# A low part made by an adding transfer, one chunk's convolution on VectorE, and a new order of work, in a gated-attention kernel

## The chip, the core and the metric

The kernel runs on one core of a Trainium2 chip. The core's engines run side by side, each from a queue of its own in program order: PE (TensorE: matrix products; its weight loads are shown as PEld), DVE (VectorE), ACT (ScalarE), POOL (GpSimd) and SP (SyncE, which here only issues transfers). They wait for one another through semaphores. SBUF is the memory on the chip that all of them read and write; PSUM is the one that PE writes into, in eight banks. The metric is the device time of one execution in microseconds (us), as the median of several.

## What is computed

A linear attention with a gated state (4 sequences, 8 heads, 768 steps, head size 48) feeds a gated projection of width 384:

```python
f = 1.0 / (1.0 + np.exp(-f_logit))
for t in range(S):
    state = f[:, :, t, :, None] * state + np.einsum('bhd,bhe->bhde', k[:, :, t], v[:, :, t])
    y[:, :, t] = np.einsum('bhd,bhde->bhe', q[:, :, t], state)
...
for k in range(K):                      # K = 5
    gate_pre += conv_w[k][None, None, :] * xp[:, k:k + S, :]
gate = 1.0 / (1.0 + np.exp(-gate_pre))
val = x @ w_val
return (gate * val @ w_out).astype(np.float32)
```

`x` is the attention's output with the heads side by side, and `xp` is `x` with four zero rows ahead of it.

## The kernel before, in words

The 768 steps are cut into six chunks of 128. For each chunk the kernel makes running sums of the gate's logarithms, exponentials of them (`exp1`, `exp2`), scaled keys and queries (`pmulk`, `pmulq`), the scores of a sequence against itself within the chunk (`scores`, from chunk 2 on `scoresq`, which leaves out a quarter that the mask makes zero), the mask (`mask`, on DVE), the product with the values (`apply`, `applyq`), the part that comes from the state (`cross`, `crossb`), and the state's update (`ktrans`, `kevac`, `dstate`, `stadd`, `stmul`). Halves of this work write to one PSUM bank from two groups of PE's rows: between the two, POOL writes one element (`mark`), which waits for PE's first group and for which PE's second group waits (`pairwise`).

`xevac` copies the attention's output from PSUM into `XF`, a buffer per chunk (two of them, in turn), with four columns ahead of it that hold the end of the chunk before (`halo`). From there the second half, the projection, starts. Its work is cut into the units of `UNITS`: units 0 and 1 are chunk 0's first and last two sequences, units 2, 3, 4 and 5 are chunks 1, 2, 3 and 4, and units 6 and 7 are the halves of chunk 5. So `mval 2 1` is output block 1 of chunk 1.

PE multiplies in a reduced 32-bit form, so each operand is split into two parts, high and low, and three of the four products are added up: high by high, high by low, low by high. For `x`, `msplit` (ACT) rounds `XF` into `xH`, and `mlow` (DVE) subtracts: `xL` = `XF` - `xH`, 128 partitions by 1536 elements for a whole chunk. `mval` (PE) multiplies both parts with the parts of `w_val` into PSUM. The gate is a convolution with five taps and a sigmoid, made in one of two ways:

- chunks 0 and 1: `conv` on PE (`mconv`), twelve small products of 32 by 32 per tap with the diagonal weights in `wd`, and then `gate` on ACT, which reads PSUM;
- from chunk 2 on: for each of three blocks of 128 channels, `mlast` (ACT) writes the last tap times `x` into `gt`, four `mtap` (DVE) add the other taps, and `gate` (ACT) makes the sigmoid in place.

`mmul` (DVE) multiplies value and gate, `mhigh` (ACT) and `mrest` (DVE) split the result, `mout` (PE) multiplies with `w_out`, and `mstore` copies to SBUF and stores.

For PE's convolution, the channels of `x` stand in turned groups of 32 (`TURN`, `place`). `CS` says from which chunk on they stand unturned: 2 before. At that chunk `halo` goes through five transfers of SP that turn the groups, elsewhere through one copy on DVE; and from it on `mval` uses a turned copy of `w_val` (`wvHt`, `wvLt`), which `wturn` makes by transfers.

The order in which all of these steps are written is a string, `PROGRAM`: every step names its chunk or unit and its part. `Ordered` gives each engine its instructions in just that order. The weights are made from 64-bit words along the way (`weight`, on POOL, ACT and DVE), and `busy` runs idle products on PE at the start.

Of the kernel before, what the change touches and what calls it, by code (L numbers as in the profile page):

```python
# [33 lines left out]
CS = 2  # L34
# [20 lines left out]
halo 0; loadf 0 0; loadf 0 1; loadq 0 0; loadv 0 0; loadk 0 0; loadk 0 1; loadk 0 2; wload 0; loadf 1 1; pexp 0 0;  # L55
loadv 0 1; pln 0 0; busy 6; cum 0 0; loadq 0 1; pexp 0 2; loadq 0 2; loadf 1 0; pln 0 2; wload 1; exp2 0 0; busy 2;
cum 0 2; exp1 0 0; pmulk 0 0; pexp 0 1; wload 2; pmulq 0 0; loadv 0 2; pln 0 1; ktrans 0 0; exp2 0 2; cum 0 1;
loadk 1 0; weight 0; loadq 1 0; scores 0 0; kevac 0 0; pmulk 0 2; loadf 2 0; exp1 0 2; dstate 0 0; mask 0 0;
exp2 0 1; ktrans 0 2; loadv 1 0; ktrans 0 3; exp1 0 1; pmulk 0 1; kevac 0 2; apply 0 0; weight 0; pexp 1 1; okc 0;
pmulq 0 1; ktrans 0 1; pmulq 0 2; xevac 0 0; scores 0 1; pln 1 1; weight 0; weight 0; weight 0; weight 0;  # L60
kevac 0 1; taps; cum 1 1; loadq 2 0; kevac 0 3; pexp 1 0; loadk 2 0; mask 0 1; pln 1 0; dstate 0 1; scores 0 2;
exp2 1 1; stadd 0 0; cum 1 0; exp1 1 1; mask 0 2; weight 2; weight 2; weight 2; apply 0 1; exp2 1 0;
weight 2; scores 0 3; weight 2; loadv 2 0; xevac 0 1; msplit 0; weight 2; dstate 0 2; loadq 2 1; exp1 1 0;
mask 0 3; weight 1; dstate 0 3; loadk 2 1; apply 0 2; weight 2; stadd 0 1; apply 0 3; weight 1; pmulk 1 0;
xevac 0 2; loadf 3 0; xevac 0 3; weight 1; ktrans 1 1; msplit 1; conv 0 0; weight 1; kevac 1 1; weight 1;
conv 0 1; pmulq 1 0; loadv 2 1; conv 0 2; pmulk 1 1; cross 1 0; pexp 2 0; weight 1; scores 1 0; okc 1; halo 1;
mlow 1; ktrans 1 0; conv 0 3; mask 1 0; weight 2; pln 2 0; conv 0 4; pmulq 1 1; scores 1 1; kevac 1 0; gate 0 2;
scan 2 0; dstate 1 1; loadk 3 0; dstate 1 0; apply 1 0; gate 0 0; mask 1 1; weight 4; gate 0 1; cross 1 1;
weight 1; ktrans 1 3; stadd 1 0; weight 4; wturn 0; scores 1 2; mlow 0; exp2 2 0; weight 4; apply 1 1;
# [10 lines left out]
applyq 2 0; mhigh 1 2; mrest 0 2; mhigh 1 1; mrest 1 2; mhigh 0 1; mrest 1 1; gate 2 2; scan 4 1; loadq 4 0;  # L80
xevac 2 1; mout 1 1; loadv 4 0; stmul 2 0; mrest 0 1; mrest 0 0; mout 1 0; pmulq 2 1; mstore 1 1; gate 2 1; mout 0 2;
xevac 2 0; okc 2; pmulq 3 0; mstore 1 0; gate 2 0; scoresq 2 2; mstore 0 2; mmul 2 1; cross 2 1; pmulq 3 1; mout 0 1;
mask 2 2; mout 1 2; mstore 0 1; scan 4 0; scoresq 2 3; mstore 1 2; mout 0 0; loadk 4 1; mask 2 3; exp2 4 0; mval 2 0;
pmulk 3 1; exp2 4 1; scoresq 3 3; pmulk 4 0; applyq 2 1; mstore 0 0; mmul 2 0; exp1 4 1; pmulk 4 1; exp1 4 0;
ktrans 4 1; mhigh 2 1; okc 4; pmulq 4 0; loadv 4 1; stmul 2 1; loadq 4 1; ktrans 3 2; ktrans 4 0; mask 3 3;
xevac 2 3; ktrans 4 2; loadf 5 0; xevac 2 2; mval 2 2; mrest 2 1; mhigh 2 0; halo 3; kevac 3 2; mrest 2 0; mlast 3 1;
mlast 3 0; mtap 3 1 0; scoresq 3 0; msplit 3; mmul 2 2; dstate 3 2; mtap 3 0 0; ktrans 3 1; ktrans 3 3; kevac 4 2;
mask 3 0; ktrans 3 0; kevac 3 1; kevac 3 3; dstate 4 2; mtap 3 0 1; kevac 3 0; dstate 3 1; mhigh 2 2; dstate 3 3;
mtap 3 0 2; dstate 3 0; kevac 4 1; scoresq 3 1; stadd 3 1; pexp 5 0; mrest 2 2; ktrans 4 3; mtap 3 0 3; loadk 5 0;
mout 2 1; mask 3 1; kevac 4 3; mlast 3 2; mlow 3; kevac 4 0; pln 5 0; mout 2 2; mtap 3 2 0; mtap 3 2 1; gate 3 0;  # L90
mval 3 0; mtap 3 2 2; mtap 3 2 3; mstore 2 2; scan 5 1; gate 3 2; mout 2 0; mstore 2 1; mmul 3 0; exp2 5 1;
scoresq 4 1; scan 5 0; dstate 4 3; dstate 4 0; cross 3 0; exp1 5 1; applyq 3 0; stadd 3 0; mtap 3 1 1; exp2 5 0;
mtap 3 1 2; exp1 5 0; mtap 3 1 3; mval 3 2; loadq 5 0; mask 4 1; xevac 3 0; loadv 5 0; gate 3 1; pmulk 5 0;
scoresq 3 2; mmul 3 2; xevac 3 1; dstate 4 1; okc 5; mhigh 3 0; check; loadk 5 1; mval 3 1; mstore 2 0; mrest 3 0;
stmul 3 0; mask 3 2; mhigh 3 2; stadd 4 0; scoresq 4 0; mmul 3 1; cross 3 1; mrest 3 2; mhigh 3 1; applyq 3 1;
mask 4 0; mrest 3 1; pmulk 5 1; mout 3 2; xevac 3 3; loadv 5 1; pmulq 4 1; xevac 3 2; loadq 5 1; mlast 4 2; halo 4;
mlast 4 1; pmulq 5 0; mout 3 1; mlast 4 0; mtap 4 1 0; stmul 3 1; mtap 4 0 0; msplit 4; mtap 4 0 1; mout 3 0;
pmulq 5 1; mstore 3 1; mstore 3 2; mlow 4; scoresq 5 0; cross 4 0; mstore 3 0; stadd 4 1; applyq 4 0; mtap 4 1 1;
mtap 4 1 2; mtap 4 1 3; mval 4 0; stmul 4 0; mask 5 0; mtap 4 2 0; xevac 4 0; gate 4 1; mtap 4 2 1; cross 5 0;
xevac 4 1; mtap 4 2 2; scoresq 4 3; mtap 4 2 3; mval 4 2; mask 4 3; gate 4 2; mtap 4 0 2; mtap 4 0 3; scoresq 4 2;  # L100
mmul 4 2; gate 4 0; count; mval 4 1; mask 4 2; mhigh 4 2; mmul 4 0; mrest 4 2; mhigh 4 0; scoresq 5 3; mmul 4 1;
cross 4 1; mrest 4 0; mhigh 4 1; applyq 4 1; mrest 4 1; mout 4 1; stmul 4 1; mask 5 3; xevac 4 2; xevac 4 3;
mout 4 2; mlast 5 2; halo 5; msplit 5; mtap 5 2 0; mtap 5 2 1; mlast 5 1; cross 5 1; mlow 5; scoresq 5 2; mstore 4 1;
mlast 5 0; mout 4 0; mstore 4 2; mask 5 2; mtap 5 2 2; mtap 5 1 0; applyq 5 1; mstore 4 0; mtap 5 1 1; mtap 5 2 3;
mtap 5 1 2; gate 5 2; mval 5 1; mtap 5 1 3; xevac 5 2; xevac 5 3; mtap 5 0 0; gate 5 1; mlast 7 2; mtap 5 0 1;
msplit 7; mval 5 0; mtap 5 0 2; mlast 7 1; mmul 5 1; mlast 7 0; mtap 7 1 0; mhigh 5 1; mlow 7; mval 5 2; mtap 5 0 3;
mrest 5 1; gate 5 0; mtap 7 2 0; mval 7 0; mmul 5 0; mmul 5 2; mhigh 5 0; mval 7 2; mtap 7 2 1; mhigh 5 2; mrest 5 0;
scoresq 5 1; mrest 5 2; mval 7 1; mtap 7 2 2; mask 5 1; mout 5 2; mtap 7 2 3; mtap 7 0 0; gate 7 2; mtap 7 0 1;
mmul 7 2; mtap 7 0 2; mhigh 7 2; applyq 5 0; mtap 7 0 3; mstore 5 2; mrest 7 2; mtap 7 1 1; gate 7 0; mtap 7 1 2;
# [31 lines left out]
def gla_moe(ctx: ExitStack, tc: tile.TileContext, q, k, f, v, wv, cw, wo, ft, out):  # L141
# [475 lines left out]
    def mhigh(w, m):  # L617
        ACT.copy(w["gH"][:, m], w["gt"][:, m])
# [291 lines left out]
```

## Time and profile before

| | |
|---|---|
| median of 3 runs | 194.4 us (193.73 to 194.59) |
| profiled execution, whole time | 193.15 us |
| its span, first to last instruction | 191.5 us |
| granted clock of PE, mean | 0.995 |
| transfers | 32.64 MB in 12522 packets |

The profile is one execution. A group row gives engine, operation, tile written and tiles read (`xL<-xf,xH`), shape and count, then the busy time in us and the mean of one in ns, then the engine's idle time ahead of it and what ended that. A row of sums by stretch gives the busy time of each engine between two times. A timeline row gives start and duration in us. In all of them a helper's line (L129, now L131) stands for every recorded operation, so rows are told apart by their tiles. PE's operations are pipelined: one record's duration overlaps the next, and what a step of PE takes is read from one start to the next.

### The profile page before, as it was taken

The page shows a single profiled execution, that of the slowest core. Times are in us where ns is not written, and L with a number is a line of the kernel's source. Part 1 is how long each engine was busy: PE and PEld are TensorE (multiplying, and loading weights), DVE is VectorE, ACT ScalarE, POOL GpSimd, SP SyncE. Part 2 cuts the span into 40 slices and gives each one's busy share as a digit, 9 for nine tenths or more (in the row PEclk, how much of TensorE's full clock was granted, in tenths as well). Part 3 has the DMA queues.
Part 4 walks back from the last instruction along what each step waited for, and adds up shares of the span by engine and source line. Part 5 has one row for each costly group of instructions (what it writes and reads, how often), then busy time and mean ns, then how long its engine had stood idle before and what let it go on. Part 6 is the DMA issues. An engine that isn't in the chain of part 4 may idle for free.

```text
span 191.5 us, 8303 instructions
## 1 busy us (share of the span) xinstructions
PE 180.2 (94%) x3706; PEld 144.8 (76%) x3706; DVE 162.2 (85%) x233; ACT 144.8 (76%) x284; POOL 13.7 (7%) x42
## 2 busy tenths in 40 slices
PE   3999999979999999999899999999999999999990
PEld 1888876667987458888698777888778778988990
DVE  7359899977998999969899997999994699998930
ACT  5889896988979998569999989394634947339440
POOL 6000110242000320000000000000000000000000
PEclk9999999999999999999999999999999999999998
DMA  5999999997647232644912308444000040010322
GB/s 194 344 419 416 416 415 409 415 349 245 203 114 285 41 113 62 206 128 135 350 48 104 113 12 266 130 183 156 15 3 3 3 167 3 3 54 4 140 87 65
DMA packets 12522, 32.64 MB, mean 170 GB/s; under 512 B 3008, under 2 KB 5440, under 8 KB 11456
## 3 DMA queue, kind: packets, MB, share of 16 engines
q1 hardware_dynamic: 12048, 31.65, 46.6%
q8 instruction: 31, 0.51, 1.2%
q10 hardware_dynamic: 432, 0.39, 0.7%
q14 instruction: 11, 0.09, 0.2%
HBM read 26.51 MB, written 4.72 MB: 163 GB/s over the span
## 4 chain that ended last, share of the span: by engine, by line
PE 56%; DVE 19%; ACT 13%; issue 6%; DMA 3%; POOL 0%; ACTq 0%; DVEq 0%
PE bk L129 49%; PE aps L129 8%; DVE re L129 7%; DVE gt L129 5%; ACT ss L129 4%; DMA out<-osb 3%; ACT e L129 2%; ACT xf L129 2%; DVE asb L129 2%; DVE qb L129 1%; DVE rg L129 1%; DVE xL L129 1%; ACT osb L129 1%; DVE rqb L129 1%; ACT re L129 1%
## 5 line engine op out<-in xcount | busy, mean ns | idle before, releaser
L129 ACT ACTIVATE e<-e 112x512 f32<-112x512 f32 (+4 forms) x38 | 36.6, 997 | 4.1 <-DMA e<-in_ft 2.0
L129 PE MATMUL bk<-rg,woH 128*128 128x512 f32 (+1 forms) x108 | 30.1, 365 | 0.1
L129 DVE TENSOR_TENSOR asb<-aps,tri 128x768 f32<-128x768 f32 (+1 forms) x24 | 24.9, 1039 | 5.4 <-PE aps L129 4.0
L129 DVE SCALAR_TENSOR_TENSOR gt<-xf,cws,gt 128x512 f32<-128x512 f32 x36 | 26.5, 748 | 1.5 <-ACT gt L129 0.9
L129 PEld LDWEIGHTS aps<-qb,kb 48*64 48x64 f32 (+1 forms) x640 | 19.9, 144 | 7.3 <-issue 4.8
L129 PE MATMUL bk<-asb,vb 128*32 128x64 f32 (+2 forms) x1280 | 24.4, 232 | 0.4 <-issue 0.4
L129 PE MATMUL aps<-qb,kb 48*64 48x128 f32 (+2 forms) x640 | 23.7, 257 | 0.1
L129 PEld LDWEIGHTS bk<-asb,vb 128*32 128x32 f32 (+1 forms) x1280 | 20.0, 108 | 4.1 <-issue 1.1
L129 PEld LDWEIGHTS bk<-rg,woH 128*128 128x128 f32 x108 | 18.6, 188 | 4.3 <-issue 0.8
L129 DVE TENSOR_TENSOR kb<-kb,e 112x1024 f32<-112x1024 f32 (+1 forms) x13 | 14.8, 1137 | 6.0 <-DMA kb<-in_k 3.5
L129 PE MATMUL bk<-rg,woL 128*128 128x512 f32 (+1 forms) x54 | 19.4, 358 | 0.0
L129 ACT ACTIVATE ss<-u,e 112x48 f32<-112x48 f32 x64 | 15.3, 324 | 3.9 <-PE bk L129 3.9
L129 DVE TENSOR_TENSOR_SCAN e<-keep,e 112x1024 f32<-112x1024 bf16 x8 | 18.3, 2282 | 0.0
L129 PE MATMUL bk<-qb,ss 48*32 48x128 f32 x640 | 15.8, 275 | 1.5 <-ACT cb L129 1.2
L129 ACT COPY osb<-bk 128x512 f32<-128x512 f32 (+1 forms) x20 | 9.8, 495 | 9.1 <-DMA out<-osb 7.3
L129 DVE TENSOR_TENSOR qb<-qb,e 112x1024 f32<-112x1024 f32 (+1 forms) x13 | 14.8, 1146 | 0.0
L129 ACT COPY xf<-bk 128x384 f32<-128x384 f32 x24 | 10.8, 473 | 4.6 <-PE bk L129 4.6
L129 PEld LDWEIGHTS bk<-qb,ss 48*32 48x32 f32 x640 | 10.6, 106 | 4.6 <-issue 1.4
L129 PE MATMUL bk<-xH,wvH 128*128 128x256 f32 (+1 forms) x36 | 13.3, 370 | 0.4 <-ACT xf L129 0.4
L129 PE MATMUL bk<-xL,wvH 128*128 128x256 f32 (+1 forms) x36 | 12.2, 339 | 0.0
L129 PE MATMUL bk<-xH,wvL 128*128 128x256 f32 (+1 forms) x36 | 12.1, 337 | 0.0
L129 ACT CAST rg<-gt 128x512 fp32r<-128x512 f32 (+1 forms) x18 | 9.3, 546 | 3.7 <-DVE gt L129 3.7
(107 smaller groups left out, 343.0 us busy)
## 6 DMA issues: line engine op xcount, KB each, us to landing
kb<-in_k SPq DMA_DIRECT2D x9, 512.0 KB, 5.2
qb<-in_q SPq DMA_DIRECT2D x9, 512.0 KB, 4.5
e<-in_f SPq DMA_DIRECT2D x4, 1024.0 KB, 10.2
vb<-in_v SPq DMA_DIRECT2D x9, 448.0 KB, 4.9
out<-osb SPq DMA_DIRECT2D x12, 256.0 KB, 2.4
raww<-in_wv SPq DMA_DIRECT2D x1, 1152.0 KB, 9.0
raww<-in_wo SPq DMA_DIRECT2D x1, 1152.0 KB, 11.8
kb<-in_k SPq DMA_DIRECT2D x1, 1024.0 KB, 14.1
```

The lines of the kernel that those rows point to most:

```text
L129: ins = emit(*a, **kw)
```

## The change

`CS` goes from 2 to 1: chunk 1's gate is no longer made by `conv` on PE but by `mlast` on ACT and `mtap` on DVE, chunk 1's `x` stands unturned, and the turning halo and the turned `w_val` serve from chunk 1 on.

For units 2 to 5 (chunks 1 to 4) `mlow` is replaced by two steps: `mneg` (ACT) writes the negative of `xH` into `xL`, and `mlowd` is a transfer, issued by POOL, that adds `XF` to it. Units 0, 1, 6 and 7 keep `mlow`. Two further functions of this kind, `mrneg` and `mrestd`, are defined and not used.

`PROGRAM` is written anew from the first step to the last. `busy` now stands three times, with 6, 3 and 3 products (6 and 2 before).

```diff
-CS = 2
+CS = 1
...
-dstate 2 1; stadd 2 1; conv 2 0; pmulq 2 0; exp1 3 1; conv 2 1; stadd 2 0; msplit 2; scan 3 0; scoresq 2 1;
...
+mask 2 0; weight 4; cross 2 0; exp2 3 1; stadd 2 1; scoresq 2 2; mlowd 2; stadd 2 0; scan 3 0; mhigh 1 1;
...
+    def mneg(w):
+        ACT.activation(w["xL"], w["xH"].bitcast(F32), AF.Copy, scale=-1.0)
+
+    def mlowd(w):
+        POOL.dma_start(w["xL"].bitcast(F32), w["xf"][:, :, w["b"], HALO:], accum_op=ALU.add)
...
+        "mneg": lambda n: mneg(view(n)), "mlowd": lambda n: mlowd(view(n)),
```

More of the change, by code (lines that the diff above doesn't have):

```diff
@@ L65 @@
[L65 to L69, printed above, removed]
@@ L80 @@
[L80 to L84, printed above, removed]
@@ L85 @@
[L85 to L109, printed above, removed]
@@ new lines @@
+gate 2 1; mtap 2 0 3; mout 0 1; mtap 2 2 0; mval 2 2; mtap 2 2 1; gate 2 0; mstore 0 1; mtap 2 2 2; xevac 2 3;
+stmul 2 1; mmul 2 1; mout 1 2; mmul 2 0; mtap 2 2 3; mout 1 0; mstore 1 2; loadf 5 0; okc 3; pmulk 3 1; xevac 2 2;
+gate 2 2; scoresq 3 0; mhigh 2 1; mmul 2 2; ktrans 3 1; mstore 1 0; mask 3 0; ktrans 3 3; mhigh 2 0; ktrans 3 0;
+mhigh 2 2; ktrans 3 2; mrest 2 0; kevac 3 0; scoresq 3 1; mrest 2 2; kevac 3 2; kevac 3 1; cross 3 0; mrest 2 1;
+kevac 3 3; loadk 5 0; dstate 3 1; mlast 3 0; mask 3 1; mout 2 1; mlast 3 2; mtap 3 0 0; msplit 3; mtap 3 2 0;
@@ new lines @@
+dstate 4 2; mneg 5; scoresq 5 1; mrest 4 0; stadd 4 1; mout 4 2; okc 5; check; mlast 5 1; mlowd 5; mlast 5 0;
+mtap 5 1 0; stmul 4 1; mtap 5 0 0; count; mout 4 0; mtap 5 1 1; mtap 5 1 2; mstore 4 2; mlast 5 2; mtap 5 1 3;
+mout 4 1; mstore 4 0; mtap 5 2 0; gate 5 1; mask 5 1; mtap 5 2 1; cross 5 1; mstore 4 1; scoresq 5 0; mtap 5 2 2;
+mtap 5 2 3; applyq 5 1; mtap 5 0 1; gate 5 2; mask 5 0; mtap 5 0 2; mval 5 2; xevac 5 2; mtap 5 0 3; xevac 5 3;
+mlast 7 2; gate 5 0; mtap 7 2 0; mlast 7 1; mtap 7 2 1; mval 5 1; mlast 7 0; mtap 7 2 2; msplit 7; mmul 5 2;
```

83 lines of the change are left out of this document (58 added, 25 removed).

## The prediction

> **What bounds the kernel now.** I read the page's busy times first, then the sums by stretch, then the tail of the timeline.
>
> ```profile
> span 191.5 us, 8303 instructions
> PE 180.2 (94%) x3706; PEld 144.8 (76%) x3706; DVE 162.2 (85%) x233; ACT 144.8 (76%) x284; POOL 13.7 (7%) x42
> 0.00:50.00 50.00, 45.25 (x812) 35.27 (x813) 39.90 (x60) 42.44 (x76) 9.47 (x24) 1.00 0.94 358
> 50.00:184.00 134.00, 132.05 (x2873) 106.78 (x2872) 122.35 (x174) 101.19 (x206) 4.27 (x18) 1.00 0.32 104
> 186.64 0.28 PE L129 MATMUL bk<-rkb,woL 128*128 128x256 f32 x1
> 182.55 0.98 DVE L129 TENSOR_TENSOR rqb<-re,rkb 128x256 fp32r<-128x256 f32 x2
> ```
>
> The sums by stretch give, after the bounds and the length, the busy time of PE, PEld, DVE, ACT and POOL, then the granted clock, the DMA share and GB/s. In the first 50 us the loads set the pace: the DMA share is 0.94 and PE idles 4.75 us. From 50 to 184 us PE is busy 132.05 of 134 us, idle 1.5%; DVE is busy 122.35 and idles 11.65 us (8.7%). The last matmul ends at 186.9, 3.4 us after DVE's last operation; then come the copy, the store and the end of the program. So from 50 us on PE is the bound, DVE comes second, and ACT third with 101.19. A change wins what it takes from PE, as long as DVE can run with less idle time than now.
>
> All sums go against the profiled execution, 193.15 us (span 191.5 and 1.65 around it). The median of the runs shown is 194.4, 1.25 above it; I add each difference to 194.4.
>
> **The change part by part.** *Chunk 1's convolution leaves PE.*
>
> ```profile
> 61.00 2.22 PE L129 MATMUL bk<-xf,wd 32*32 32x512 f32 x48
> L129 PE MATMUL bk<-xf,wd 32*32 32x512 f32 x240 | 11.0, 597 | 0.0
> L129 DVE SCALAR_TENSOR_TENSOR gt<-xf,cws,gt 128x512 f32<-128x512 f32 x36 | 26.5, 748 | 1.5 <-ACT gt L129 0.9
> L129 ACT ACTIVATE gt<-xf,cws 128x512 f32<-128x512 f32 x9 | 6.2, 720 | 0.1
> L129 DVE TENSOR_TENSOR xL<-xf,xH 128x1536 fp32r<-128x1536 f32 x4 | 8.1, 2020 | 0.0
> L129 ACT CAST xH<-xf 128x1536 fp32r<-128x1536 f32 x4 | 5.9, 1465 | 0.0
> ```
>
> Ten `conv` steps, five of chunk 0 and five of chunk 1, make 240 records and 11.0 us; half goes, 5.5 us. The timeline row agrees: two steps (48 records) take 2.22 us. PE in the second stretch falls to 132.05 - 5.5 = 126.55; with its present 1.5% of idle time that is 128.5 us in place of 134, 5.5 less.
>
> DVE gets 12 taps at 0.748 = 9.0 us. ACT gets 3 first taps (`mlast`) at 0.72 = 2.2; its three gates stay, and so does the count of table loads, 8 in both programs. *The low part leaves DVE.* Four subtractions of 128x1536 go, 8.1 us; ACT gets four negated copies of that size, which I price as the CAST of the same shape: 4 x 1.465 = 5.9. All this lies in the second stretch: DVE 122.35 + 9.0 - 8.1 = 123.25; ACT 101.19 + 2.2 + 5.9 = 109.3, which fits under 128 us and is charged nothing. If that cover fails, a negated copy delays the exponentials and casts queued behind it on ACT by its 1.465 us.
>
> So DVE must now do 123.25 in about 128.5, 4.1% idle, where it idles 8.7% today. How dense can it run?
>
> ```profile
> 100.00:140.00 40.00, 39.64 (x935) 31.69 (x937) 38.41 (x51) 30.92 (x63) 0.62 (x7) 1.00 0.35 118
> 60.00:140.00 80.00, 78.45 (x1904) 61.37 (x1902) 75.14 (x93) 65.67 (x130) 3.82 (x13) 1.00 0.41 134
> 50.00:100.00 50.00, 48.49 (x1110) 38.33 (x1109) 46.22 (x57) 43.78 (x87) 3.20 (x6) 1.00 0.48 149
> ```
>
> In the 40 us where it already does two chunks' taps, it idles 4.0%; in the 80 us from 60, 6.1%; in the 50 us from 50, 7.6%. At 4.0% the stretch takes 128.4, at 6.1% 131.3. The new work resembles the first row but also falls into the second; I take 5%: 129.7, or **-4.3**, with bounds -5.6 and -2.7.
>
> On DVE, from the mask ahead of the low part on, chunk 1 stood so before (`gt` and `rg` are the gate's tiles, `kb`, `qb` the keys and queries, `e` the decays):
>
> ```order
> L129 TENSOR_TENSOR asb<-aps,tri_72 128x768
> L129 TENSOR_TENSOR xL<-xf_91,xH 128x1536
> L129 TENSOR_TENSOR asb<-aps,tri_72 128x768
> L129 TENSOR_SCALAR okc<-e_79 112x16
> L129 TENSOR_TENSOR kb_67<-kb_67,e_82 112x1024
> ```
>
> And now, ahead of its gate products:
>
> ```order
> L131 TENSOR_TENSOR kb_67<-kb_67,e_82 112x1024
> L131 TENSOR_TENSOR asb<-aps,tri_72 128x768
> L131 SCALAR_TENSOR_TENSOR gt<-xf_91,cws,gt 128x512 x6
> L131 TENSOR_TENSOR qb_65<-qb_65,e_79 112x1024
> L131 SCALAR_TENSOR_TENSOR gt<-xf_91,cws,gt 128x512 x5
> L131 TENSOR_TENSOR gt<-bk_107,gt 128x512
> ```
>
> The `xL` row is gone, and eleven taps stand almost in one block of 8.2 us. What queues behind them on DVE is the next mask, for which PE's `applyq` waits; the third part of chunk 1 has its last tap behind two products.
>
> *The transfer that adds* is in no row of the trace; nor is any DMA that POOL issues. It moves 768 KB and must also read its destination.
>
> ```profile
> out<-osb SPq DMA_DIRECT2D x12, 256.0 KB, 2.4
> e<-in_f SPq DMA_DIRECT2D x4, 1024.0 KB, 10.2
> DMA to landing us min/median/max: 4.9/10.2/17.8
> ```
>
> From below its time L is 2.4 us, the row of a third of its size. From above, counted as 1536 KB at in_f's median, it is 15.3. The two longest of in_f's four fell into the full queue of the first stretch; the shortest, 4.9 us for 1024 KB, is nearest to stretches with a DMA share of 0.35, and gives 7.3 for 1536 KB. I take 7.3. [...]
>
> What PE has to do between each transfer's place in the table of steps and the first `mval` that reads `xL` covers it. PE's steps, from the starts in the timeline:
>
> ```profile
> 57.24 1.32 PE L129 MATMUL bk<-ident,kb 112*128 112x112 f32 x12
> 59.42 1.64 PE L129 MATMUL bk<-vb,ksb 128*48 128x48 f32 x64
> 71.46 1.87 PE L129 MATMUL bk<-asb,vb 64*32 64x64 f32 x128
> 74.29 0.51 PE L129 MATMUL bk<-rg,woH 128*128 128x256 f32 x2
> 75.47 0.40 PE L129 MATMUL bk<-rg,woH 128*128 128x256 f32 x2
> 78.12 0.90 PE L129 MATMUL aps<-qb,kb 48*64 48x128 f32 x32
> 78.95 0.67 PE L129 MATMUL bk<-qb,ss 48*32 48x128 f32 x32
> 79.55 0.50 PE L129 MATMUL bk<-rg,woH 128*128 128x256 f32 x2
> 146.75 0.73 PE L129 MATMUL bk<-rg,woH 128*128 128x512 f32 x2
> 148.96 0.62 PE L129 MATMUL bk<-rg,woH 128*128 128x512 f32 x2
> ```
>
> `applyq` 74.29 - 71.46 = 2.83; a half `mout` 75.47 - 74.29 = 1.18, a whole one 148.96 - 146.75 = 2.21; `scoresq` 0.83; `cross` 0.60; `ktrans` 0.44; `dstate` 0.41. Chunk 1: `scoresq`, `applyq`, three half `mout`, `scoresq` = 8.0. Chunk 2: `mout`, `scoresq`, three `dstate`, `cross`, `scoresq` = 5.7. Chunk 3: two `scoresq`, `mout`, three `ktrans`, two `cross`, `applyq` = 9.2. Chunk 4: two `mout`, `cross`, `scoresq`, `applyq` = 8.7. At 7.3 only chunk 2's is late, by up to 1.6, less what PE still has in hand when it is issued: **+0.5** (0 to 1.6).
>
> POOL's queue behind the last weight step, before:
>
> ```order
> L129 TENSOR_TENSOR woL<-ca_103,woH 128x576
> L129 TENSOR_TENSOR woL<-ca_101,woH 128x576
> L129 MEMSET mark 1x1 x15
> ```
>
> and now:
>
> ```order
> L131 TENSOR_TENSOR woL<-ca_101,woH 128x576
> L131 MEMSET mark 1x1
> L131 DMA xL<-xf_91 128x12x128
> L131 MEMSET mark 1x1 x4
> L131 DMA xL<-xf_90 128x12x128
> L131 MEMSET mark 1x1 x2
> L131 DMA xL<-xf_91 128x12x128
> L131 MEMSET mark 1x1 x5
> L131 DMA xL<-xf_90 128x12x128
> L131 MEMSET mark 1x1 x3
> ```
>
> The marks tell PE that the first group of rows has left a bank. A transfer waits for ACT's negated copy, and the marks behind it wait too, with PE's second group behind them.
>
> ```profile
> L129 POOL MEMSET mark<- x18: 89/89/168, 32.4 to 170.7; 1x1 f32 x18
> ```
>
> The copies stand well ahead on ACT and the marks cost 0.09 us each, so I charge nothing; in chunk 1 `applyq` needs its mark some 2 us after the transfer may start, and any issue time above that would be paid once.
>
> *The rest.* CS = 1 sends chunk 1's halo, not chunk 2's, through five small SP transfers; they sit between loads of the same kind, the taps wait for them, and I charge nothing. Four more idle matmuls in the first stretch, up to 0.625 each (8 of them are 3.8 us of PE's row below), stand where PE idles 4.75 us: **+0.4** (0 to 2.5). The new order of the loads may win or lose some of that idle time; I take 0.
>
> ```profile
> L129 PE MATMUL bk<-idle 128*128 128x512 bf16 x8 | 3.8, 625 | 3.0 <-DVE bk L129 3.0
> ```
>
> Sum: -4.3 + 0.5 + 0.4 = -3.4: span 188.1, profiled execution 189.75, median **191.0**, faster by 1.7%.
>
> **The rivals.** *PE alone decides*: DVE idles 4%, nothing is late, the idle matmuls are free: -5.5, 188.9; the first stretch could add 1.4 (30% of its idle time), 187.5. For it: PE's 1.5%. Against: DVE's 8.7%.
>
> *DVE takes over*: it idles 7.6%, as in the 50 us where chunk 1's taps arrive: 133.4, -0.6 + 0.9 = 194.7, no change.
>
> *The transfer comes late and PE waits*, the slow side: it decides from an L of about 9.1, where the lateness of the four chunks equals PE's 5.5 - 0.4. At in_f's median, 10.2, it is 2.2 + 4.5 + 1.0 + 1.5 = 9.2, so +4.1, 198.5. For it: in_f's median. Against: the DMA share of 0.35 later on.
>
> *DVE is not relieved*, because POOL's issue of the transfer shuts it out:
>
> ```profile
> 65.58 2.82 DVE L129 TENSOR_TENSOR xL<-xf,xH 128x1536 fp32r<-128x1536 f32 x1
> 65.36 1.42 POOL L129 TENSOR_TENSOR woL<-ca,woH 128x576 fp32r<-128x576 f32 x1
> 100.85 1.75 DVE L129 TENSOR_TENSOR xL<-xf,xH 128x1536 fp32r<-128x1536 f32 x1
> ```
>
> Beside a POOL operation `xL` took 2.82, alone 1.75. Four times 1.07 makes DVE 127.5; at 5% idle 134.2, +0.2 + 0.9 = 195.5. [...]
>
> **How the numbers follow.** Forecast 0.50 (its own range 189.8 to 192.7), PE alone 0.17, DVE takes over 0.10, late transfer 0.15, DVE not relieved 0.08. 187.5 to 196.0 holds all but the late transfer. Within 0.5%, about what a measurement of this kernel can tell from no change, is 193.4 to 195.4: the third case and a little of the fifth, 0.12. Faster 0.67; slower 0.21.
>
> **What would show it.** In the profile after: 120 `wd` records and not 240; PE's busy time about 5 us lower, DVE's about 1 higher and its share of 50 to the end at 94 to 96%; the transfer landing within 8 us, and no wait of PE on `xL` over 1.6. A transfer above 9 us, marks that come late behind it, or DVE idling over 7% would make it wrong.

## The result and the profile after

The changed kernel took 200.08 us (median of 4 runs, 199.19 to 201.01) against 194.5 of the kernel before on the same chip (4 runs, 193.73 to 194.78): a ratio of 1.0342, 95% interval 1.0288 to 1.0396. It is slower by 3.4%, where 191.0 us and 1.7% faster were forecast. The profiled execution took 200.48 us. Six of the profiled executions used further down (e2, e5, e7, e9, e10, e15) were longer than their kernel's median by 0.7 to 1.5%, so mainly the places of gaps and the DMA rows are read from them.

From the page of the changed kernel: busy time, the granted clock in 40 slices of 4.97 us, TensorE's row of the convolution, the queue that GpSimd's transfers use (packets, MB, share of 16 engines), a queue of kind "instruction", and the transfers' time to landing.

```profile
span 198.8 us, 8093 instructions
PE 178.8 (90%) x3589; PEld 145.9 (73%) x3590; DVE 162.9 (82%) x241; ACT 151.1 (76%) x291; POOL 21.3 (11%) x46
PEclk9999999999999996699999999998799999999999
L131 PE MATMUL bk<-xf,wd 32*32 32x512 f32 x120 | 4.9, 592 | 0.1
q0 software_dynamic: 6208, 3.15, 14.4%
q8 instruction: 30, 0.49, 1.1%
xL<-xf POOLq DMA_DIRECT2D x4, 768.0 KB, 9.6
```

The work moved as written: 120 `wd` records, VectorE 162.9 us where it had 162.2. But PE is busy only 1.4 us less and idles 20.0 us of its span, where it idled 11.3. And the clock has two dents that the kernel before didn't have, in the slices from 75 to 85 us and from 134 to 144 us.

Sums by stretch of the changed kernel (after the bounds and the length: PE, PEld, DVE, ACT, POOL, granted clock, DMA share, GB/s) put the loss in two places:

```profile
64.00:72.00 8.00, 5.72 (x260) 4.59 (x256) 8.00 (x13) 6.39 (x15) 3.53 (x4) 1.00 0.53 109
72.00:78.00 6.00, 3.27 (x49) 2.87 (x48) 1.06 (x2) 3.46 (x11) 0.00 (x0) 0.86 1.19 168
78.00:86.00 8.00, 8.00 (x179) 6.59 (x179) 5.31 (x8) 4.49 (x7) 0.09 (x1) 0.68 0.52 186
132.00:142.00 10.00, 7.28 (x238) 5.87 (x237) 6.76 (x8) 7.25 (x12) 0.26 (x3) 0.83 0.39 81
```

From 64 to 78 us PE idles 5.0 of 14 us, and from 132 to 142 it idles 2.7. Taken by single microseconds, the granted clock is 0.50 in each of them from 77 to 83 and from 138 to 141. At half speed a clock of 0.86 over 6 us and 0.68 over 8 us means (0.84 + 2.56) / 0.5 = 6.8 us; 0.83 over 10 us means 3.4. While the clock is halved, PE is busy, but at half its rate: the wide products of `mval` start 0.43 us apart in the first dent (79.90 and 80.33) and 0.23 us apart after the second (141.53 and 141.76). Who was waited for? Four of the six waits of the changed kernel's PE (us in total, times, longest):

```profile
PE bk L131 <- issue: 6.6, 7, 2.7
PE aps L131 <- issue: 3.1, 2, 2.7
...
PE bk L131 <- ACT e L131: 1.9, 3, 1.2
...
PE bk L131 <- DMA xL<-xf: 0.4, 1, 0.4
```

"issue" is time in which the engine waited for nothing that the profile shows. In the kernel before that row has 1.2 us, the longest 0.4. PE hardly ever waited for the transfer to land (0.4 us). Its timeline shows where it stood still, in the middle of a step:

```profile
64.65 0.44 PE L131 MATMUL bk<-qb,ss 48*32 48x128 f32 x13
66.27 0.62 PE L131 MATMUL bk<-qb,ss 48*32 48x128 f32 x19 [1.18 <-issue]
66.82 0.90 PE L131 MATMUL aps<-qb,kb 48*64 48x128 f32 x32
67.65 1.25 PE L131 MATMUL bk<-asb,vb 64*32 64x64 f32 x77
70.00 0.91 PE L131 MATMUL bk<-asb,vb 128*32 128x64 f32 x51 [1.10 <-issue]
70.72 0.78 PE L131 MATMUL bk<-qb,ss 48*32 48x128 f32 x32
...
73.78 0.89 PE L131 MATMUL aps<-qb,kb 48*64 48x128 f32 x26
77.40 0.48 PE L131 MATMUL aps<-qb,kb 48*64 48x64 f32 x6 [2.73 <-issue]
...
133.35 1.27 PE L131 MATMUL bk<-asb,vb 64*32 64x64 f32 x69
137.35 1.34 PE L131 MATMUL bk<-asb,vb 128*32 128x64 f32 x59 [2.73 <-issue]
```

Count between the gaps. From 66.27 to the next gap: 19 + 32 + 77 = 128 matmuls. From 70.00: 51, 32, 18 of `mout` (the rows left out) and 26 make 127, with one record missing. A matmul comes with its weight load (3589 and 3590 records), so that is 256 instructions. The packets of q8, the queue of kind "instruction", are 16 KB each, and there are 30 of them for PE's 7179 recorded matmuls and weight loads, about one for each 256 instructions. Read packet by packet from the trace (start to end, us):

```
resumed 66.27   packet 67.37 - 68.56   resumed 70.00
resumed 70.00   packet 75.00 - 75.95   resumed 77.40
boundary 132.49   packet 134.85 - 135.78 resumed 137.35
```

(132.49 is 128 matmuls ahead of the gap at 134.6.) In these three PE goes on 1.4 to 1.6 us after the end of the packet. At 66.27 the packet started 1.1 us after the boundary, at 70.00 it started 5.0 us after. The first transfer was issued at 67.53 and landed at 79.23. The DMA queues of the changed kernel between 69 and 75 us (packets, MB, share of 16 engines) and between 75 and 77 us:

```profile
q0 software_dynamic: 1310, 0.67, 102.8%
```

```profile
q0 software_dynamic: 224, 0.11, 70.9%
q1 hardware_dynamic: 51, 0.21, 44.8%
q8 instruction: 1, 0.02, 3.0%
```

The slices of this view are empty up to 70.1 us and full from there on: for about five of the six microseconds all 16 engines moved nothing but the adding transfer's packets of about half a KB, and not one packet of instructions came through. That is **theory F**: PE's instructions come by DMA, 256 at a time, and wait behind the transfer; where PE works off 128 matmuls sooner than the next packet comes (2.6, 4.7 and 2.1 us at these three boundaries), it runs dry, and with the gap its clock is halved for a while (0.50 from 76.3 to 83.1 us, beginning while PE still stood, and from 137.8 to 141.2). Rivals: **O**, the new order packs small matmuls too densely, whatever the transfer does; **L**, the transfer's landing or the delay of other transfers comes late; **P**, each transfer costs a fixed amount wherever it runs; **D**, a wait for data that the profile doesn't show.

### The profile page after: what moved, and what is told of

Read it like the earlier page. It is cut to its first block, busy times and chain, and to the rows that moved or that the text cites. A ratio compares the mean times of both kernels' runs of the same rounds, so it can differ in the third digit from the quotient of the medians.

```text
span 198.8 us, 8093 instructions
## 1 busy us (share of the span) xinstructions
PE 178.8 (90%) x3589; PEld 145.9 (73%) x3590; DVE 162.9 (82%) x241; ACT 151.1 (76%) x291; POOL 21.3 (11%) x46
## 3 DMA queue, kind: packets, MB, share of 16 engines
q0 software_dynamic: 6208, 3.15, 14.4%
## 4 chain that ended last, share of the span: by engine, by line
PE 57%; ACT 14%; DVE 12%; DMA 8%; issue 7%; ACTq 0%; DVEq 0%
PE bk L131 49%; PE aps L131 8%; DVE re L131 7%; DMA xL<-xf 5%; ACT e L131 4%; DMA out<-osb 3%; ACT gt L131 2%; DVE gt L131 2%; ACT xH L131 1%; ACT xL L131 1%; DVE asb L131 1%; ACT osb L131 1%; DVE rg L131 1%; ACT ss L131 1%; ACT xf L131 1%
## 5 line engine op out<-in xcount | busy, mean ns | idle before, releaser
L131 DVE SCALAR_TENSOR_TENSOR gt<-xf,cws,gt 128x512 f32<-128x512 f32 x48 | 35.0, 749 | 3.4 <-ACT gt L131 2.5
L131 DVE TENSOR_TENSOR asb<-aps,tri 128x768 f32<-128x768 f32 (+1 forms) x24 | 24.9, 1039 | 11.7 <-PE aps L131 11.5
L131 PE MATMUL bk<-rg,woH 128*128 128x512 f32 (+1 forms) x108 | 31.0, 373 | 0.0
L131 PE MATMUL aps<-qb,kb 48*64 48x128 f32 (+2 forms) x640 | 24.5, 258 | 3.5 <-issue 3.1
L131 PEld LDWEIGHTS aps<-qb,kb 48*64 48x64 f32 (+1 forms) x640 | 20.4, 144 | 8.6 <-issue 6.2
L131 PEld LDWEIGHTS bk<-asb,vb 128*32 128x32 f32 (+1 forms) x1280 | 19.4, 109 | 8.4 <-issue 5.2
L131 PEld LDWEIGHTS bk<-rg,woH 128*128 128x128 f32 x108 | 19.3, 195 | 3.9 <-issue 0.4
L131 POOL MEMSET mark<- 1x1 f32 x18 | 2.3, 126 | 103.8 <-PE bk L131 103.8
L131 DVE SCALAR_TENSOR_TENSOR re<-xf,cws,re 128x256 f32<-128x256 f32 x24 | 11.3, 482 | 1.6 <-ACT re L131 1.1
L131 PEld LDWEIGHTS bk<-rg,woL 128*128 128x128 f32 x54 | 10.6, 196 | 1.6
```

What stands on the lines that cost most here:

```text
L131: ins = emit(*a, **kw)
```

## The experiments

Ratios are to the kernel before on the same chip, with 95% intervals.

### Without the transfer, and with a landing that nobody waits for

In e1 the line of the transfer is taken out; TensorE's instructions are the same as in the changed kernel.

```
-        POOL.dma_start(w["xL"].bitcast(F32), w["xf"][:, :, w["b"], HALO:], accum_op=ALU.add)
+        pass
```

> Leaves out the adding transfers of chunks 1 to 4 (the low part there is then only the negated copy, not the difference); order and all other work as in the changed kernel. Theory F (TensorE's instructions arrive by DMA in 16 KB packets of 256 instructions, and these wait behind the transfer's packets, so TensorE runs dry in runs of small matmuls and its clock is then halved for a few us): the two 2.73 us gaps at 74.67 and 134.62 go (5.5 us) and with them the two stretches at half clock (6.8 and 3.4 us long, about 5 us lost), 200.1 - 10.5 = 189.6 us (188 to 192); the 1.2 and 1.1 us gaps at 65.1 and 68.9 may stay, since they begin before the transfer's packets run. Rival O (the new order itself packs small matmuls too densely, whatever the transfer does): the 2.7 us gaps stay, 198 us or more. Rival L (the transfer delays stores and loads, so ScalarE and VectorE come late): 190 us too, but then PE in the changed kernel should have waited for them, and a transfer into a spare tile tells.

In e2 it adds into a spare tile, which GpSimd sets to zero once near the start:

```
+        POOL.dma_start(spare, w["xf"][:, :, w["b"], HALO:], accum_op=ALU.add)
```

> As the changed kernel, but the four transfers add into a spare tile that nobody reads (the low part is then only the negated copy): the same packets at the same time, but no step of TensorE waits for their landing. Theory F: still 200 us (198.5 to 201.5), with the two gaps of over 2 us and the half clock in their places, since it is the packets and not the landing that cost. Rival L in the form in which the landing of xL is late for mval: 190 us, as without the transfer. Rival O: 198 to 201.

In e3 `mneg n` is dropped and `mlowd n` becomes `mlow n` for n = 2 to 5.

> The changed kernel's order, with the low part of chunks 1 to 4 subtracted by VectorE again, where the transfer stood (no negated copy, no transfer). Theory F: no gap of over 2 us, no half clock; VectorE has 8.1 us more in a stretch in which it idled about 12 us, so 191 to 195 us, below the changed kernel by 5 us or more and near the kernel before. Rival O: 198 us or more.

Measured: e1 190.84 us, 0.9903 (0.9863 to 0.9943); e2 196.3 us, 1.0159 (1.0074 to 1.0243); e3 195.24 us, 1.0093 (1.0043 to 1.0143). PE's issue rows of e1:

```profile
PE bk L131 <- issue: 2.2, 5, 1.2
PE aps L131 <- issue: 0.2, 1, 0.2
```

Without the transfer both 2.7 us gaps are gone, and 4.4% of the time; O in its strong form falls. The gap of 1.2 us in `cross` at 64.6 stays, as F has it. There is no adding transfer in e1, but other DMA work surrounds that gap; between 60 and 65 us its queues are:

```profile
q1 hardware_dynamic: 248, 1.45, 86.6%
q8 instruction: 1, 0.02, 1.1%
```

The 128 matmuls ahead of the gap ran in 3.3 us, and the packet started 2.1 us after the boundary, in place of 1.1 us behind 66.27 in the changed kernel. So this gap goes with ordinary loads, and not with small matmuls alone. In e2, where no step waits for the landing, a gap of 2.73 us is still there at 75.2 and one of 1.88 at 103.2, and 2.6% over e1 is lost; that is the packets. The other 1.8% up to the changed kernel fell short of F's "still 200". The gap at 134.6 was missing in e2 (0.99 us on a semaphore at 135.6), with the transfer issued 0.6 us earlier; the trace speaks for the moment. PE reached this boundary at 134.8 in e2 and at 132.5 in the changed kernel; in e2 the transfer had landed at 134.6, and the packet ran at once, from 134.8 to 135.8. e3 says that the order with four subtractions is about 1% slower than the kernel before: VectorE has 169.1 us to do. F's range of 191 to 195 us for e3 was missed by a little.

### The same bytes in larger packets

> The four transfers copy in place of adding (the low part is then x itself): the same bytes from the same tile into the same tile. Theory F sets the price by the time that the packets hold the DMA engines: if the adding makes them slow (9.6 us to landing, packets of about 0.5 KB), a copy lands in 5 to 6 us with larger packets and the gaps shrink by half, 193 to 196 us; if the copy has the same packets and takes as long, 200 us. Rival O: 198 us or more either way.

e4 drops `accum_op`, so the low part there is x itself. e7 adds from the tile `xH`, which has no halo, and so gives zero:

```
+        POOL.dma_start(w["xL"].bitcast(F32), w["xH"].bitcast(F32), accum_op=ALU.add)
```

> The four transfers still add, but from the tile xH, which lies without gaps, in place of xf, whose rows of 512 B are set apart by the halo (the low part is then zero). If the 6208 packets of about 0.5 KB come from the rows of the source, packets become large, the landing comes down from 9.6 towards the plain copy's 5.5 us and theory F expects 0.99 to 1.00 of the kernel before; if they come from the adding itself, packets and landing stay, and so does the time, 1.016 to 1.035.

Measured: e4 191.52 us, 0.9916 (0.9878 to 0.9954), below the 193 to 196 that F gave; e7 192.44 us, 0.9932 (0.9894 to 0.9971). The transfers' rows, of e4 and then of e7:

```profile
q0 software_dynamic: 832, 3.15, 5.5%
xL<-xf POOLq DMA_DIRECT2D x4, 768.0 KB, 5.5
```

```profile
q0 software_dynamic: 576, 3.15, 8.8%
xL<-xH POOLq DMA_DIRECT2D x4, 768.0 KB, 6.6
```

All three move 3.15 MB. Adding from `xf` makes 6208 packets, 1552 each transfer: 128 partitions times 12 rows of 512 B are 1536. A plain copy from the same rows makes 832, adding from a tile without gaps 576. Time follows the packets: landing in 9.6, 5.5 and 6.6 us, and a ratio of 1.034, 0.992 and 0.993. So it is neither the adding nor the bytes, but adding row by row. A smaller delay is left in e7: a gap of 1.64 us at 73.9, its packet 5.0 us after the boundary, with the adding transfer at 84% of the engines.

### Which transfers cost

e5 keeps the transfers of steps 3 and 5, e6 those of steps 2 and 4; the other two chunks are subtracted by VectorE.

> Of the four adding transfers only those of steps 3 and 5 (chunks 2 and 4) are kept, which in the changed kernel ran beside wide matmuls with no gap of over 0.5 us; steps 2 and 4 are subtracted by VectorE. Theory F (the loss is a coincidence of the transfer with a run of small matmuls): no gap over 2 us on TensorE, 1.00 to 1.015 of the kernel before, like the order with four subtractions (1.0093) or below it, since VectorE has 4 us less. Rival P (each transfer costs its share, about 2.4 us of the 9.3, wherever it runs): 1.009 + half of (1.034 - 1.009) = 1.022.

> The other half: only the transfers of steps 2 and 4 (chunks 1 and 3) are kept, those of steps 3 and 5 are subtracted by VectorE. Theory F: the gaps of over 2 us at about 75 and 135 us and the half clock behind them stay, 1.025 to 1.04 of the kernel before. Rival P: 1.022, the same as the other half.

Measured: e5 193.48 us, 1.0022 (0.9982 to 1.0063); e6 202.2 us, 1.045 (1.0364 to 1.0535). Twice two transfers of the same size, 4.3% apart: P falls, and the loss lies where F put it. e6 has the gaps again, at 74.1 (1.91 us) and 135.0 (2.55), e5 has no gap over 0.94 us near its transfers. It has one of 2.28 us at 65.6, with no adding transfer near: the packet started 3.1 us after the boundary, behind loads and stores. e6 is even slower than all four transfers (1.0342), a little above F's 1.025 to 1.04. In part that is another wait: PE waits 2.1 us at 109.2 for VectorE's mask, as in e3, which subtracts on VectorE too (2.0 us).

### GpSimd subtracts

> The low part of chunks 1 to 4 is subtracted by GpSimd, where the transfer was issued (no negated copy, no transfer). From the 1.42 us of GpSimd's subtraction of 128x576 elements, 128x1536 takes about 3.8 us, 15 us in all on an engine with 14 us of work. Theory F: no gap over 2 us; 0.99 to 1.01 of the kernel before if GpSimd and VectorE do not hinder one another, about 1.03 if VectorE loses the time that GpSimd takes (15 us, of which it has some 10 idle).

Measured: 203.27 us, 1.0529 (1.0452 to 1.0606). No gap of PE on issue over 0.8 us, but another bound, and above the 1.03 that F allowed for it. Four subtractions of VectorE (`mrest`) that take 1.41 us in the changed kernel took 4.65 beside GpSimd's; the first row is VectorE's, the second GpSimd's:

```profile
67.37 4.65 DVE L131 TENSOR_TENSOR rg<-gt,rg 128x256 fp32r<-128x256 f32 x4
...
66.19 4.88 POOL L131 TENSOR_TENSOR xL<-xf,xH 128x1536 fp32r<-128x1536 f32 x1
```

One of the four took 3.66 us in place of 0.42 (67.69 to 71.35); it ended when the subtraction had ended (71.07). That is the prediction's rival of VectorE shut out, here by an operation and not by an issue. PE waited 1.8 us for a mark that stood behind the subtraction in GpSimd's queue.

### A correct version with large packets

e9 first copies x into a tile without gaps; e10 does so for steps 2 and 4 alone.

```
     def mneg(w):
+        ACT.copy(xc, w["xf"][:, :, w["b"], HALO:])
         ACT.activation(w["xL"], w["xH"].bitcast(F32), AF.Copy, scale=-1.0)
...
+        POOL.dma_start(w["xL"].bitcast(F32), xc, accum_op=ALU.add)
```

> ScalarE first copies x of the chunk into a tile xc without the halo gaps (1.5 us more per chunk on ScalarE, 6 us in all on an engine that idles about 48 us), and the transfer adds from xc. The result is the reference's. Theory F: packets as with the contiguous source (576 in place of 6208, landing about 6.6 us), so the time is that run's 0.993 of the kernel before, 0.99 to 1.00 if ScalarE's 6 us are hidden, up to 1.01 if the longer wait of the transfer's issue behind ScalarE shows. Rival P (any adding transfer costs 2.4 us): 1.03.

> As the run before, but only steps 2 and 4 (chunks 1 and 3, which run beside small matmuls) go through xc; steps 3 and 5 keep the transfer in rows of 512 B. Theory F: 0.99 to 1.00 of the kernel before, since steps 3 and 5 cost nothing that can be measured and ScalarE has 3 us less than with four copies. Rival P: 1.01 or more.

Measured: e9 196.51 us, 1.0142 (1.0079 to 1.0205); e10 197.07 us, 1.0191 (1.0134 to 1.0248). Both missed. The packets did what was expected in e9 (576, landing 6.5 us), and it is 2% better than the change, but 2% worse than e7 with the same packets and 6 us less of ScalarE. Its profile has gaps on issue at other places (2.15 us at 101.3, before the second transfer was issued at 102.54). In the profiled executions PE's issue rows make 8.6 us in e9 and 6.2 in e7, and 6.8 us run at half clock in place of 3.4. So most of the difference again looks like PE without instructions; why the gaps lie elsewhere is open.

### The transfers in the kernel before

e11 issues four transfers from `xf` into a spare tile, each behind its `mlow`.

> The kernel before, with four adding transfers from xf (rows of 512 B) into a spare tile that nobody reads, issued by GpSimd behind the subtraction of each of chunks 1 to 4. Theory F: the kernel before has the convolution of chunk 1 or wide matmuls among the small ones, so that TensorE rarely empties its instructions within a transfer: 1.00 to 1.012 of the kernel before, gaps of at most 1.5 us. Rival P (2.4 us for each transfer wherever it runs): 1.045 or so.

Measured: 195.91 us, 1.0159 (1.009 to 1.0228). A third of the 4.4% that the transfers cost in the changed kernel, so P's 1.045 fails; but more than the 1.012 that F allowed. PE's issue row went from 1.2 us to 2.6 (longest 0.9), the span by 2.5; the other 1.1 us is mostly found in two rows of e11:

```profile
ACT osb L129 <- DMA out<-osb: 10.5, 4, 4.3
...
PE bk L129 <- ACT xf L129: 1.6, 2, 1.3
```

In the kernel before they have 7.3 and 0.6 us. ScalarE waited 3.2 us more for stores to land and was 2.0 us late at 92 us, where PE then waited for it. That is L, by way of the stores.

### Useless work where PE ran dry

e12 puts `fill 10`, ten idle matmuls into a tile that is written anew behind them, ahead of `scoresq 2 3` and of `applyq 4 0`.

> The changed kernel with its four transfers, and ten useless wide matmuls (128x512, about 0.22 us each, 2.2 us) ahead of each of the two places where TensorE ran dry (scores of step 2, output of step 4); they write a PSUM tile that is written anew behind them. Theory F: 20 instructions take the place of the wait, the gaps go from 2.73 us to about 0.5, and without the gap the clock may not be halved: 1.01 to 1.034 of the kernel before, no longer than the changed kernel in spite of 4.4 us more work. Rival (TensorE waits there for data or is bound by its own work): 4.4 us are added, 1.057.

Measured: 203.39 us, 1.0519 (1.0455 to 1.0583): by the total a miss. The timeline of e12 at the first place:

```profile
73.64 2.33 PE L131 MATMUL aps<-idle 128*128 128x512 bf16 x10
75.90 1.19 PE L131 MATMUL aps<-qb,kb 48*64 48x128 f32 x32
...
78.19 0.39 PE L131 MATMUL bk<-xH,wvH 128*128 128x512 f32 x1
79.26 0.50 PE L131 MATMUL bk<-xL,wvH 128*128 128x512 f32 x1 [0.69 <-DMA xL<-xf]
```

The `mval` begins at 78.19 here and at 79.90 in the changed kernel: with 2.33 us more to do, PE is 1.7 us earlier. A wait for data would not have shrunk. At the second place `mval` begins at 138.37 in place of 139.54. Then it lost all of it: new gaps of 1.45 us at 147.8 and 1.83 at 165.7, and a halved clock at 169 (0.986 in the mean of the execution). Twenty more matmuls had moved every later boundary.

### Only the boundaries moved

e13 and e14 cut the 12 idle matmuls near the start into 4 and 8 narrow ones of the same width together: 36 and 84 more matmuls ahead, nothing else.

```
-            PE.matmul(free[-1][:], idle[:, 0:128], idle[:], start=True, stop=True)
+            for x in range(0, B * C, 128):
+                PE.matmul(free[-1][:, x : x + 128], idle[:, 0:128], idle[:, x : x + 128], start=True, stop=True)
```

> The changed kernel with each of its 12 idle wide matmuls near the start cut into four narrow ones of together the same width: 36 more matmuls ahead of everything else, so that each boundary between two packets of 256 instructions lies 36 matmuls earlier in the program; from 60 us on the work and its order are the same. Theory F (counted from the trace: packets of 128 matmuls, resumed at 66.27, 70.00 and 77.42): the second boundary falls into the output matmuls at about 72 us, behind 128 matmuls nearly all small that run in under 3 us, so the gap stays or grows (2.7 to 4 us, at about 72 in place of 74.7), and near 133 a gap of about 2.6 us stays: 1.03 to 1.05 of the kernel before. Rival D (TensorE waits for data, or the order is slow in itself): 1.034 unchanged, gaps in the old places.

> As the run before with each idle matmul cut into eight: 84 more matmuls ahead, all boundaries 84 matmuls earlier. Theory F: one boundary falls to the end of the output of step 2 (70.6 us), and the 128 matmuls behind it hold wide ones that last until about 78 us, about as long as the slowed packet needs: no gap over 1.3 us between 72 and 80 us and no half clock there; the gap of about 2 us near 134 stays. 1.00 to 1.02 of the kernel before, though not one step of the work has moved. Rival D: 1.034, gaps in the old places.

Measured: e13 206.75 us, 1.0758 (1.0692 to 1.0824); e14 208.3 us, 1.0779 (1.0688 to 1.087). The first `mval` starts at 48.26 in the changed kernel, 48.00 in e13 and 49.29 in e14, so the start isn't it. Timeline of e13:

```profile
68.48 1.72 PE L131 MATMUL bk<-asb,vb 128*32 128x64 f32 x87 [1.92 <-issue]
69.95 1.18 PE L131 MATMUL bk<-qb,ss 48*32 48x128 f32 x32
71.06 0.80 PE L131 MATMUL bk<-rg,woH 128*128 128x256 f32 x2
...
75.33 0.28 PE L131 MATMUL bk<-rg,woL 128*128 128x256 f32 x1 [2.37 <-issue]
...
135.68 1.48 PE L131 MATMUL bk<-asb,vb 128*32 128x64 f32 x95 [2.85 <-issue]
```

The gap moved from the scores at 74.7 into the output matmuls at 73.0, 36 matmuls earlier, and the second one likewise, from 134.6 to 132.8: both places as F counted them, the sizes not (2.37 us where it had 2.7 to 4, and 2.85 where it had 2.6). After the second gap the clock stayed whole (1.00 from 120 to 145 us). In e14 the gap left the stretch from 72 to 76, and PE came to its `mval` before the transfer had landed:

```profile
75.77 0.40 PE L131 MATMUL bk<-xH,wvH 128*128 128x512 f32 x1
77.86 0.50 PE L131 MATMUL bk<-xL,wvH 128*128 128x512 f32 x1 [1.69 <-DMA xL<-xf]
...
168.49 1.09 PE L131 MATMUL bk<-asb,vb 128*32 128x64 f32 x41 [3.28 <-issue]
```

But a new one of 3.28 us opened in the fourth transfer, and 3.19 at 134.1. D falls, since only the boundaries have moved. F's counts of the places held (but for the 1.69 us, which is L), though the gap at 134.1 was to be about 2 us; its totals, 1.03 to 1.05 and 1.00 to 1.02, didn't, since it had counted only two boundaries of nearly thirty.

> A try for a version that beats both: transfers for steps 3 and 5 alone (1.0022 before), with the boundaries 84 matmuls earlier. Theory F: the gap of 2.28 us at 65.6 us and the 6.8 us of half clock behind it change place or shrink; if they go, 0.98 to 0.99 of the kernel before, if the run of small matmuls from 61 to 71 us makes another gap of the kind, 1.00. Rival D: 1.002.

e15, e5 with the cut into eight: 200.78 us, 1.037 (1.0312 to 1.0428), where F had 0.98 to 1.00. The gap of 2.28 us at 65.6 shrank to 1.12, but one of 3.1 us opened at 160.0, at the end of the transfer of step 5 (151.1 to 160.6) that had cost nothing in e5.

### The control: the same cut without a transfer

> The kernel before (no transfer), with its 8 idle wide matmuls cut into eight each: 56 more matmuls ahead, all boundaries of the instruction packets 56 matmuls earlier. Theory F: without the transfer a packet comes about 3.5 us after the boundary before it, so a boundary anywhere costs at most about 1.2 us where small matmuls stand close: 0.995 to 1.01 of the kernel before. Rival Q (the cutting of the idle matmuls itself costs, by the start or by the clock): 1.04, as the changed kernel lost by it.

> The changed kernel's order with four subtractions by VectorE and no transfer (1.0093 before), the idle matmuls cut into eight: boundaries 84 matmuls earlier, as in the split of the changed kernel that came to 1.078. Theory F: 1.00 to 1.025, since no packet waits behind a transfer. Rival Q: 1.05.

Measured: e16 201.25 us, 1.0427 (1.0336 to 1.0519); e17 197.65 us, 1.0254 (1.0179 to 1.0329). The kernel before, whose work wasn't touched, lost as much as the change costs, and F's 0.995 to 1.01 for it was missed; e17 lies at the edge of F's 1.00 to 1.025. By the ratio this spoke for Q, that the cutting itself costs. Hence e18: each idle matmul in seventeen pieces, 128 more in all, which is one whole packet, so that the boundaries fall where they fell before.

```
+            for x in range(0, 448, 64):
+                PE.matmul(free[-1][:, x : x + 64], idle[:, 0:128], idle[:, x : x + 64], start=True, stop=True)
+            for x in range(10):
+                PE.matmul(free[-1][0:32, 448:464], idle[:, 0:32], idle[:, 0:16], start=True, stop=True)
```

> The kernel before, each of its 8 idle matmuls cut into seven of 64 columns and ten of 16 columns (seventeen in place of one): 128 more matmuls ahead, which with their weight loads are 256 instructions, just one packet, so that all boundaries fall again where they fell in the kernel before. Theory F: the gaps of about 1 us between 87 and 178 us go and the time comes back, 0.995 to 1.01 of the kernel before. Rival Q (many cut idle matmuls cost by themselves): 1.04 or more, since there are more of them than in the cut that came to 1.043.

Measured: 195.63 us, 1.0132 (1.0093 to 1.0171), a little above F's range. PE's issue row of e16; then the issue row and the first scores of e18; then the same two of the kernel before:

```profile
PE bk L129 <- issue: 7.9, 7, 1.9
```

```profile
PE bk L129 <- issue: 2.0, 4, 0.7
...
15.30 0.94 PE L129 MATMUL aps<-qb,kb 48*128 48x128 f32 x12
```

```profile
PE bk L129 <- issue: 1.2, 4, 0.4
...
11.51 1.16 PE L129 MATMUL aps<-qb,kb 48*128 48x128 f32 x16
```

e16's span is 6.5 us longer than the kernel before, and its issue row 6.7: the whole loss of this profiled execution (the shortest of e16's runs, 199.64 us) is PE without instructions, in seven gaps of 0.9 to 1.9 us between 87 and 178 us, with no adding transfer anywhere. Beside most of them the DMA engines were nearly idle: the packet started 0.6 to 0.9 us after the boundary and PE went on about 3.2 us after it, but its 128 matmuls took only 2.2. There small matmuls alone are enough. e18 has more pieces, so many that its first scores come 3.8 us later, and yet it ends only 2.6 us later: its issue row is back at 2.0. The place of the boundaries decides, not the cutting.

The longest gap without an adding transfer is in e17:

```profile
PE bk L131 <- issue: 6.1, 5, 2.5
```

It lies in a run of small matmuls, from 79.3 to 81.8 us. The packet started 2.3 us after its boundary, and from 72 us until then ordinary loads and stores held 77% of the engines. So ordinary transfers seem to keep packets waiting too; beside the adding transfer the wait was longest, 5.0 us.

## Why the prediction was wrong

**The convolution off PE, -5.5**: about right. 120 records went. PE's busy time fell from 180.2 to 175.4 in e1 and to 175.8 in e4 (4.8 and 4.4 us). In the changed kernel (178.8) the halved clock put most of it back.

**VectorE at 5% idle, -4.3**: its work came out as forecast (162.9 for 162.25 + 0.9). How dense it could run the changed kernel doesn't show, because PE ran dry. The runs without that loss do: from 50 us to its last operation VectorE idles 6.4% in e1 and 6.1% in e4, against 8.4% in the kernel before and the 5% assumed. So it ran denser, though not as dense as forecast. The bound on PE's idle time was the unsound part: "its present 1.5%" was a property of where the packet boundaries fall in the kernel before, and e16 takes it to 4.3% more time without touching the work.

**The transfer, +0.5: the step that failed.** The prediction asked only whether the low part lands ahead of its `mval`. Even there L was short: 9.6 us median, 11.7 the longest, in place of 7.3. But the lateness it feared was 0.4 us of PE's waits. What it left out is what else those DMA engines carry: 6208 packets kept all 16 busy for about 7 us each time (14.4% of 198.8 us, divided by four), and PE's instructions stood behind them. With these boundaries the transfer costs 1.0342 - 0.9903 = 4.4% of the kernel before, 8.5 us, or 198.8 - 189.4 = 9.4 by the spans of the two profiled executions. Of the 9.4 the two gaps are 5.5 and the halved clock (6.8 + 3.4, against 3.4 in e1) some 3.4 of PE's busy time, 178.8 against 175.4.

**The rival "transfer late, PE waits"**, 198.5, had the right sign and nearly the size, by the wrong mechanism. As a wait it was small or absent where PE ran dry (0.4 us in the changed kernel), and larger where PE came earlier: 1.69 us in e14, 1.39 in e13, 0.69 in e12. e6 has both, gaps and 0.9 us of it.

**POOL's marks, nothing**: right. The issue took 1.8 us of GpSimd each time, and no gap of PE ends on a mark; where `applyq` of step 2 stood still (1.10 us at 68.9), it stood at a packet's boundary and waited for no semaphore.

**VectorE shut out by the issue, 195.5**: not seen. VectorE's operations beside the issue at 67.53 took 1.41 us for four, where e8's subtraction made them 4.65.

**Start, +0.4**: first scores at 12.88 us against 11.51, so 1.4 us late by the new order of the loads and steps; PE's first 50 us have 43.47 us of work in place of 45.25. This is part of why even e1 and e4 gain 1% and not the 2% that the sum without a transfer gave. In e1 PE does 4.8 us less but idles 2.7 us more than in the kernel before (14.0 and 11.3): its issue rows went from 1.2 to 2.4 us, it waits 2.2 us for the decays `e` from ScalarE, a wait that the kernel before doesn't have, and the first scores come 0.8 us later (12.34 for 11.51).

Of the signs named, three pointed the right way: PE's busy time not 5 us lower, the transfer above 9 us, VectorE idle 12.9% (122.82 busy of the 141 us from 50 to 191).

On the instructions: the packets of q8 are 16 KB each, one for about 256 of PE's instructions, and PE's waits on issue came to 9.7 us in the changed kernel and 7.9 in e16, against 1.2 in the kernel before. On the clock: in the changed kernel it stood at 0.50 for 6.8 and for 3.4 us. What brings such a stretch on isn't settled here: 3.4 us at half followed a gap of 1.20 us in e1 (mean clock 0.991), and none followed 2.85 us in e13 (1.00 from 120 to 145 us) and 2.54 in e17 (1.00 in every sum up to 180 us). So the part of theory F that a gap halves the clock holds for the changed kernel, not as a rule.

What stays open: why the gaps of e9 and e10 lie elsewhere than those of e7, what halves the clock after one gap and not after another, and how much of the new order's own 1% (e3) is only the place of its boundaries. e17 has the same order at 1.0254 with others. No version beat both kernels: e5 is level with the kernel before (1.0022), e1, e4 and e7 are faster by 0.7 to 1% but don't compute the low part. An order that places wide matmuls behind each boundary on purpose was not tried.

## What to carry to other kernels

Ask of a new transfer not only when it lands but what shares its engines: count packets, not bytes (the same 3.15 MB came to 1.034 in 6208 packets, to 0.992 in 832 and to 0.993 in 576), and look for the engine with the densest instructions: here PE's 7179 recorded ones came in 30 packets, by theory F over the engines that the transfer filled. A gap in the middle of a step whose releaser is "issue" is a sign; count the instructions between two such gaps. And where a kernel stands at 1 to 2% of idle time, a difference of a few per cent between two orders may be the place of the packet boundaries (4.3% in e16, with the work untouched): shift them (by a number of empty instructions, and by one whole packet as a control) before a cause is believed.

## What the runs showed of the hardware

- An adding transfer whose source lies in rows of 512 B became a packet for each row: 6208 packets of about 74 ns (14.4% x 16 x 198.8 us / 6208). A plain copy of the same rows made 832 packets of about 201 ns (5.5% x 16 x 190.1 / 832), and adding from a tile without gaps 576 of about 471 ns.
- Where 128 small matmuls took 2 to 3.3 us, PE ran dry without any such transfer: 1.2 us in e1, up to 1.9 in e16 and 2.5 in e17 (loads and stores held 87% of the DMA engines in e1 from 60 to 65 us, and 77% in e17 from 72 to 79.5). At the three boundaries read above PE resumed 1.4 to 1.6 us after the packet's last byte.
- Moving the boundaries of unchanged work took the kernel before from 1 to 1.043, and the changed kernel from 1.034 to 1.076 and 1.078.
- A packet of instructions that started 1.1 us after its boundary at 66.27 started 5.0 us after the next, while the adding transfer filled the engines (102.8% over 69 to 75 us). Beside ordinary loads and stores it was 2.1 to 3.1 us (e1, e5, e17), beside nearly idle engines 0.6 to 0.9 (e16).
- GpSimd's subtraction of 128x1536 stretched four operations of VectorE from 1.41 to 4.65 us.
